# A decode block's tail: w_down with columns as output, the last V piece in two parts, and w_up in one load

## The chip, the cores and the metric

The kernel runs on one core of a Trainium2 chip. The metric is the device time of one execution in microseconds (us), smaller being better. Runs of the kernel before gave 657.47, 657.50 and 658.03 us; the median is 657.5.

## The reference

One token goes through an attention block with a cache of 65,536 positions (32 query heads on 8 key/value heads, 128 per head) and then through a gated layer, both with a residual:

```python
def _A_ref(x, k_cache, v_cache, wq, wo):
    q = (x @ wq).reshape(B, Sq, 32, 128).transpose(0, 2, 1, 3)
    k, v = jnp.repeat(k_cache, 4, axis=1), jnp.repeat(v_cache, 4, axis=1)
    p = _softmax(jnp.einsum("bhqd,bhkd->bhqk", q, k) * 128 ** -0.5)
    o = jnp.einsum("bhqk,bhkd->bhqd", p, v)
    return o.transpose(0, 2, 1, 3).reshape(B, Sq, 4096) @ wo

def _B_ref(x, w_gate, w_up, w_down):            # 512 -> 1792 -> 512
    g, u = x @ w_gate, x @ w_up
    return (_sigmoid(g) * u) @ w_down

h = x + _A_ref(_layernorm(x), k_cache, v_cache, wq, wo)
h2 = h + _B_ref(_layernorm(h), w_gate, w_up, w_down)
```

All inputs and the output of 512 numbers are bf16. The caches are 268 MB of the 282 MB that one execution reads.

## The kernel before

**The stream.** SP issues nearly all loads, in one queue and in a fixed order (L331 to L361): wq, then for each of the eight heads three pieces of K and three of V (12, 8 and 12 chunks of 2048 positions) into a ring of 32 chunks in SBUF, and at the end w_out, the last V pieces, w_gate, w_up and w_down. An issue that has a name in its dependence list waits until the engine that reads the old content of those chunks is done. The last V piece of the last head comes in two loads (`LAST`, L318: chunks 20 to 28 and 28 to 32). Then SP waits for the first six rounds of the last head's PV (L356) and issues w_gate once, w_up twice (three quarters and one quarter, `W_SPLIT`) and w_down three times (`WD_SPLIT`: rounds 0 to 7, 8 to 11, 12 and 13; a round is 128 of the 1792 rows).

**Heads.** DVE transposes K chunks (L511), PE makes scores (L535), DVE takes maxima, ACT the exponentials (L557), DVE transposes these (L567), and PE multiplies them with V in "rounds": one round is two chunks, eight matmuls on four column groups of the array (`pv`, L587). PE's program is a loop written out by hand with registers and branches (`pe_flow`, L669): block `sums` computes the addresses of a round from registers (L582), issues its eight matmuls (section `B`, all through the helper at L430), counts down `m` (L735, L736), and at its end goes on (L738) to `waits` when `k` is not zero. `waits` (L718) sets `m` to the rounds still left, waits for the next V load and goes back to `sums`. A branch that is taken from there for the last piece of V is `fourth` (L727), and for the last head `last_rounds` (L728), which waits for the load of chunks 28 to 32. So the last piece of V of the last head runs four rounds, then `waits`, then two rounds.

**After the heads.** The last head's output is scaled (L600), picked out (L603), regrouped (L616 to L625) and multiplied with the last four rows of w_out, in column form (`project`, L627): the weights are 128x128 slices of w_out with a column stride of four, the moving operand is one column of O, and y comes out as 128 partitions x 4. There follow the residual (L804), the layer norm's sums (L391) and hc, the centred input (L805); its scale, rstd, comes by a short chain on DVE and POOL (L396 to L402). w_gate and w_up are applied in row form on the four column groups (L818): 16 matmuls each, with 448 columns per group. ACT takes tanh of the gate (L825), DVE makes sg2 (L826), the product hh (L828) and its 32x32 transposes hhT (L831), whose columns 32r are the inputs of w_down's round r.

**w_down in row form.** For each of 14 rounds and four column groups, one column of hhT is the weight and 128 columns of w_down move past it (L836); the result is four rows of 128 on partitions 0, 32, 64 and 96. The residual enters the same accumulation by one fp32 matmul (L823) of `gsel`, a selection matrix made at the start (POOL memset L366, DVE reduction L380), with `hz`, a copy of h spread over columns (L807). Two casts on DVE and two on ACT gather the four rows on partition 0 (L840 to L845), and SP stores one row of 512 (L846).

Of the kernel before, what the change touches and what calls it, by code (L numbers as in the profile page):

```python
# [6 lines left out]
bf16 = mybir.dt.bfloat16  # L7
fp32 = mybir.dt.float32
# [5 lines left out]
HKV = 8  # L14
GS = 4
NQ = 32
DH = 128
# [198 lines left out]
def bass_sequential_preLN__gqa_block_cached__glu_gated_glu__decode_kernel(  # L216
# [17 lines left out]
    RW = 4  # L234
    WD_SPLIT = [(0, 8), (8, 12), (12, 14)]
    FG = FF // 4

    with ExitStack() as es:
        def sb(name, shape, dt):
            return es.enter_context(nc.sbuf_tensor(name, shape, dt))  # L240

        gsel = sb("gsel", [128, 128], fp32)
        hz = sb("hz", [128, 128], fp32)
        identf = sb("identf", [128, 128], fp32)
# [27 lines left out]
        qh = sb("qh", [32, 512], bf16)  # L272
        qt = sb("qt", [32, 512], bf16)
        hT = [sb(f"hT{i}", [128, 4], fp32) for i in range(2)]
# [18 lines left out]
        hhT = sb("hhT", [128, FG], bf16)  # L293
        y_sb = sb("y_sb", [1, D], bf16)

# [53 lines left out]
        for i, cols in enumerate(LAST):  # L349
            load("V", h, 2, (), ("vb", "vl")[i], f"V{h}.2{('', 'b')[i]}", cols)  # L350
        for k, w in (("wg", B_w_gate), ("wu", B_w_up)):
# [13 lines left out]
        for nm, t, v in (("onesf", onesf[:, :], 1.0), ("xz0", xz[:, :], 0.0), ("onef", one_f[:, :], 1.0), ("nhalf", nhalf[:, :], -0.5),  # L365
                         ("gs0", gsel[:, :], 0.0), ("zcol", zcol[:, :], 0.0), ("qh0", qh[:, :], 0.0), ("qz0", qz[:, :], 0.0),  # L366
                         ("PTz", PT_sb[:, 4 * 512:PT_ROW], 0.0), ("Wz", ktw[:, W0:KTW_ROW], 0.0)):
            op("pool", lambda e, t=t, v=v: e.memset(t, v), name=nm)
# [101 lines left out]
        op("act", lambda e: e.activation(ps(1, 0, 512, 0, 8), bass.AP(tensor=zcol, offset=0, ap=[[1, 8], [0, 512]]), AF.Copy), ["zcol"], "zq")  # L470
        op("pe", project_q, ["zq", "xz", "wq", "identf", "lsel", "onef", "sel", "gsel", "row", "PTz", "qz0"], "q")
        op("act", lambda e: e.activation(  # L472
# [113 lines left out]

        def pv(h, r, rounds=0):  # L587
            P.part["pe"] = ("B", (h, r, rounds))
            rounds, name = rounds or PARTS[r], f"PV{h}.{r}" + "a" * (rounds == 6)
# [79 lines left out]
        def pe_flow(e, section):  # L669
            later = []  # L670

            def away(op, reg_, value, name, body, back=None):
                getattr(e, op)(reg_, value, on_true=name, on_false=f"{name}_not")
                later.append((name, body, back or f"{name}_not", blocks[-1][0]))
                label(f"{name}_not")

# [41 lines left out]
            def waits():  # L718
                e.reg_alu(m, k, 0, ALU.add)
                e.reg_mov(k, 0)  # L720
                e.br_eq(w, w0, on_true="second", on_false="fourth")
# [5 lines left out]
                e.br_ne(i, i_last, on_true="sums", on_false="last_rounds")  # L727
                label("last_rounds", "fourth")  # L728
                section("VL")

            section("B")
# [5 lines left out]
            label("sums_end")  # L737
            away("br_ne", k, 0, "waits", waits, "sums")  # L738

            away("br_eq", w, w0 - 12, "outs", lambda: section("O"))  # L740
            goto("next", "part")
# [24 lines left out]
        for i in range(HKV + 1):  # L766
            loop, last = 0 < i < HKV, i == HKV
            for r in range(NR):
# [5 lines left out]
                if i and r == 0:  # L774
                    transposed(i - 1)
                    P.part = {"pe": ("V0", i), "dve": ("B0", i) if loop else None}
                    denominators(i - 1)
                    op("pe", lambda e: None, [f"V{i - 1}.0", f"z{i - 1}"])
                    if last:
                        pv(i - 1, r, 6)  # L780
                    P.part["pe"] = ("L" if last else "V2", i)
                    if last:
                        project7()
                        columns()
                    op("pe", lambda e: None, [f"V{i - 1}.1"])
                    pv(i - 1, r, 4 if last else 0)
                if i and r == 3:
                    P.part["pe"] = ("V3", i)
                    op("pe", lambda e: None, [f"V{i - 1}.2"])
                    if last:  # L790
                        P.part["pe"] = ("VL", i)
                        op("pe", lambda e: None, [f"V{i - 1}.2b"])
                    pv(i - 1, r)
                    P.part["pe"] = ("O", i)
                    head_out(i - 1)
                if not last and r == 3:
# [9 lines left out]
                                                   op0=ALU.mult, op1=ALU.add), ["tot.1"], "hc")  # L806
        op("dve", lambda e: e.tensor_tensor(hz[:, :].rearrange("p (j k) -> p j k", k=4),  # L807
                                            bass.AP(tensor=sel_f, offset=0, ap=[[32, 128], [1, 32], [0, 4]]),
                                            bass.AP(tensor=hT[1], offset=0, ap=[[4, 128], [0, 32], [1, 4]]), ALU.mult),
           ["hT.1", "self"], "hz")  # L810
        ln_rstd(1, STB, 0, 4.0)
        wd_v = ring[:, AT["wd"] * CH:AT["wd"] * CH + NF * D].rearrange("p (r n) -> p r n", r=NF)
        for i, (nm, bank) in enumerate((("wg", GB), ("wu", UB))):
            at = W_AT[nm]
            for kt in range(4):
                for c in range(4):
# [11 lines left out]
        op("dve", lambda e: e.tensor_tensor(hh[:, :].rearrange("p (r q) -> p r q", r=NF),  # L828
                                            ps(UB, 0, FG).rearrange("p (q r) -> p r q", r=NF),
                                            sg2[:, :].rearrange("p (q r) -> p r q", r=NF), ALU.mult), ["gu1", "sg2"], "hh")  # L830
        op("dve", lambda e: e.transpose(hhT[:, :], hh[:, :]), ["hh"], "hhT")  # L831
        for i, (r0, r1) in enumerate(WD_SPLIT):
            for r in range(r0, r1):
                for g in range(4):
                    last = r == NF - 1 and g == 3
                    op("pe", lambda e, r=r, g=g: e.matmul(  # L836
                        ps(YB, 0, 128, 32 * g, 32 * g + 1), lhsT=hhT[:, 32 * r:32 * r + 1], rhs=wd_v[:, r, g * 128:(g + 1) * 128],
                        start=False, stop=(r == NF - 1), tile_position=(0, 32 * g), skip_group_check=True),
                       ["hhT", f"wd{i}"] if r == r0 and g == 0 else (), "y" if last else None)
        for g in (0, 2, 1, 3):  # L840
            if g < 2:
                op("dve", lambda e, g=g: e.tensor_copy(y_sb[:, 128 * g:128 * g + 128], ps(YB, 0, 128, 32 * g, 32 * g + 1)), ["y"], f"ysb{g}")
            else:
                op("act", lambda e, g=g: e.activation(y_sb[:, 128 * g:128 * g + 128], ps(YB, 0, 128, 32 * g, 32 * g + 1), AF.Copy),
                   ["y"], f"ysb{g}")  # L845
        dma("sp", lambda e: e.dma_start(out[0], y_sb[:, :]), "out", [f"ysb{g}" for g in range(4)], "out")  # L846
        P.at_end = ("out",)
# [29 lines left out]
```

## Time and profile before

| What | us | Where from |
|---|---|---|
| median of three runs | 657.5 | times |
| the profiled execution | 657.62 | times |
| its span, first to last instruction | 656.2 | page |
| PE busy | 436.0 | page |
| DVE busy | 351.2 | page |
| ACT busy | 42.8 | page |
| last V load of chunks 28 to 32, issue to landing | 38.5 | DMA issues |
| w_up, second part, issue to landing | 34.3 | DMA issues |
| w_down, last part, issue to landing | 37.2 | DMA issues |
| start of the output's DMA issue | 654.99 | timeline |

The profile is of one execution. Times in it count from the first instruction. A row of the timeline gives start, duration, engine, line, operation, output and input, how many instructions it merges, and in brackets how long the engine was idle before it and what ended that. "PEq" is PE's sequencer, which runs branches and register work; "PEld" is the load of weights. A matmul's end is modelled. The granted clock of TensorE changes in steps during the execution; its mean is 0.775 of full speed.

### The profile page before, as it was taken

What the parts mean: (1) busy time and instruction counts of PE and PEld (TensorE: products, weight loads), DVE (VectorE), ACT (ScalarE), POOL (GpSimd) and SP (SyncE); (2) the same over time, 40 slices, a digit from 0 to 9 for tenths busy, and PEclk for the clock granted to TensorE, in tenths of its full rate; (3) what the DMA queues carried; (4) which work ended last, traced back from release to release, by engine and by line L of the source; (5) the groups of instructions that cost most, each with busy time, mean ns of one, the idle gap of its engine ahead of it and who ended that gap; (6) DMA issues with size and microseconds to landing.
All of it is one profiled execution on the core that took longest, in us unless ns stands there. A gap on an engine that the chain in (4) does not pass through costs nothing.

```text
span 656.2 us, 6248 instructions
## 1 busy us (share of the span) xinstructions
PE 436.0 (66%) x2316; PEld 69.4 (11%) x1548; DVE 351.2 (54%) x436; ACT 42.8 (7%) x114; POOL 3.6 (1%) x17
## 2 busy tenths in 40 slices
PE   2698675838658457776676477594667856775855
PEld 1100010001001010010100110010100101001212
DVE  3498836847266645647258380674536572573102
ACT  1100200020000200011000200002000020002001
POOL 1000000000000000000000000000000000000000
PEclk9798688767689587796677676985877967877777
DMA  9999999999999999999999999999999999999998
GB/s 400 431 447 431 425 424 446 437 434 426 441 431 431 431 431 442 437 434 423 423 443 431 431 437 445 437 437 431 415 431 431 431 434 434 457 431 411 439 422 341
DMA packets 8386, 282.33 MB, mean 430 GB/s; under 512 B 961, under 2 KB 962, under 8 KB 1474
## 3 DMA queue, kind: packets, MB, share of 16 engines
q1 hardware_dynamic: 8354, 282.33, 99.6%
q10 hardware_dynamic: 32, 0.00, 0.0%
HBM read 282.33 MB, written 0.00 MB: 430 GB/s over the span
## 4 chain that ended last, share of the span: by engine, by line
DMA 65%; PE 19%; DVE 12%; issue 3%; ACT 1%; SPq 0%; PEldq 0%
DMA ring<-in_A_k_cache_dram 34%; DMA ring<-in_A_v_cache_dram 23%; PE PS L430 18%; DVE ktw L511 11%; DMA ring<-in_B_w_down_dram 6%; DMA ring<-in_A_wq_dram 2%; ACT P_sb L557 1%; DVE PT_sb L567 0%; DVE M_sb L518 0%; SPq L355 0%; PE PS L551 0%; PE PS L544 0%; PEldq L171 0%; SPq L360 0%; PE PS L572 0%
## 5 line engine op out<-in xcount | busy, mean ns | idle before, releaser
L511 DVE STREAM_TRANSPOSE ktw<-ring 128x1024 f32<-128x1024 f32 x256 | 292.4, 1211 | 170.5 <-DMA ring<-in_A_k_cache_dram 170.5
L430 PE MATMUL PS<-ktw 128*128 128x512 bf16 x1024 | 293.2, 438 | 114.8 <-DVE ktw L511 106.7
L430 PE MATMUL PS<-ring,PT_sb 128*32 x1024 | 102.7, 506 | 65.4 <-PEq L171 45.1
L430 PEld LDWEIGHTS PS<-ktw 128*128 x256 | 27.2, 106 | 370.4 <-issue 258.1
L600 ACT ACTIVATE po_sb<-PS,rl 128x512 bf16<-128x512 f32 x8 | 5.5, 687 | 522.2 <-PE PS L430 522.2
L430 PEld LDWEIGHTS PS<-ring,PT_sb 128*32 x1024 | 20.7, 116 | 144.3 <-issue 142.8
L518 DVE TENSOR_REDUCE M_sb<-PS 128x1 f32<-128x512 f32 x32 | 19.9, 684 | 20.0 <-PE PS L430 20.0
L546 DVE TENSOR_REDUCE gmj<-PS 1x4 f32<-1x128 f32 x8 | 2.2, 278 | 40.2 <-PE PS L544 40.2
L557 ACT ACTIVATE P_sb<-PS,negmax 128x512 bf16<-128x512 f32 x32 | 21.5, 685 | 0.3
L567 DVE STREAM_TRANSPOSE PT_sb<-P_sb 128x512 bf16<-128x512 bf16 x32 | 20.2, 688 | 1.7 <-ACT P_sb L557 1.7
L430 PE MATMUL PS<-ring,xz 128*8 x32 | 10.0, 490 | 3.6 <-DMA ring<-in_A_wq_dram 3.6
L616 DVE TENSOR_TENSOR Lw<-O,blk_of 128x896 bf16<-128x896 bf16 (+1 forms) x2 | 1.4, 682 | 19.9 <-ACT O L606 19.9
L544 PE MATMUL PS<-identf,gm 128*1 128x128 f32 x16 | 4.5, 380 | 5.5 <-issue 3.4
L551 PE MATMUL PS<-one_f,gmrep 1*128 1x1 f32 x16 | 4.7, 358 | 5.0 <-DVE gmrep L548 5.0
L574 DVE TENSOR_REDUCE lsum<-PS 128x1 f32<-128x4 f32 x8 | 1.3, 162 | 11.9 <-PE PS L572 11.9
L475 DVE STREAM_TRANSPOSE qt<-qh 32x512 bf16<-32x512 bf16 x1 | 0.7, 699 | 12.7 <-ACT qh L472 12.7
L430 PE MATMUL PS<-ktw,O 128*1 x26 | 7.5, 457 | 0.0
L557 ACT ACTIVATION_READ_ACCUMULATOR P_sb<-PS,negmax 128x1 f32 x32 | 6.5, 203 | 0.0
L603 PE MATMUL PS<-sel_bf,po_sb 128*128 128x4 bf16 x32 | 2.1, 170 | 6.3 <-ACT po_sb L600 6.3
L411 PE MATMUL PS<-xs,xpick 16*128 16x32 bf16 x1 | 0.2, 202 | 7.5 <-DMA xs<-in_A_x_dram 7.5
L572 PE MATMUL PS<-L_sb,lsel 128*128 128x4 f32 x16 | 2.5, 229 | 3.8 <-DVE PT_sb L567 3.8
L661 DVE COPY yr<-PS 1x512 f32<-1x512 f32 x1 | 0.7, 678 | 8.1 <-PE PS L659 8.1
(88 smaller groups left out, 71.6 us busy)
## 6 DMA issues: line engine op xcount, KB each, us to landing
ring<-in_A_k_cache_dram SPq DMA_DIRECT2D x16, 6144.0 KB, 25.4
ring<-in_A_v_cache_dram SPq DMA_DIRECT2D x15, 6144.0 KB, 25.7
ring<-in_A_v_cache_dram SPq DMA_DIRECT2D x9, 4096.0 KB, 30.6
ring<-in_A_k_cache_dram SPq DMA_DIRECT2D x8, 4096.0 KB, 24.7
ring<-in_A_wq_dram SPq DMA_DIRECT2D x1, 4096.0 KB, 12.3
ktw<-in_A_wo_dram SPq DMA_DIRECT2D x1, 3584.0 KB, 14.9
ring<-in_A_v_cache_dram SPq DMA_DIRECT2D x1, 2048.0 KB, 38.5
ring<-in_B_w_gate_dram SPq DMA_DIRECT2D x1, 1792.0 KB, 30.8
```

Of the source, the lines that this page charges most:

```text
L430: return e.add_instruction(mybir.InstMatmult(name=nc.get_next_instruction_name(), engine=mybir.EngineType.PE, ins=[rhs, lhsT], outs=[e.low ...
L511: op("dve", lambda e, d=dst, sr=src: e.transpose(d, sr), deps, f"T{b}.{c}", to="T")
L518: op("dve", lambda e, u=u: e.tensor_reduce(M_sb[:, u % 4:u % 4 + 1], ps(u % NS, 0, 512), AX.X, ALU.max), [f"S{b}.{NC - NR + k}"], f"mx{u}" ...
L544: op("pe", lambda e: e.matmul(ps(MISC, 0, 128, 0, 1), lhsT=gm[:, :], rhs=identf[:, :], start=True, stop=True), [f"gm{h}"], f"gmT{h}", to="Q")
L546: op("dve", lambda e: e.tensor_reduce(gmj[:, :], ps(MISC, 0, 128, 0, 1).rearrange("p (i a c) -> p a i c", a=4, c=NC), AX.XY, ALU.max), [f" ...
L551: op("pe", lambda e: e.matmul(ps(MISC, 128, 129), lhsT=gmrep[0:1, :], rhs=one_f[0:1, 0:1], start=True, stop=True), [f"gmrep{h}"], f"neg{h}")
L557: op("act", lambda e, b=b: e.activation(P_sb[:, (b % 4) * 512:(b % 4 + 1) * 512], ps(b % NS, 0, 512), AF.Exp, bias=negmax[:, k:k + 1], sca ...
L567: op("dve", lambda e, b=b: e.transpose(PT_sb[:, (b % 4) * 512:(b % 4 + 1) * 512], P_sb[:, (b % 4) * 512:(b % 4 + 1) * 512]), [f"E{b}"], f" ...
L572: op("pe", lambda e: e.matmul(ps(MISC, 132, 136), lhsT=lsel[:, :], rhs=L_sb[:, :], start=True, stop=True), [f"PT{NR * h + NR - 1}"], f"l{h ...
L600: op("act", lambda e: e.activation(po_sb[:, :], ps(PO, 0, 512), AF.Copy, scale=rl[:, :]), [f"PV{h}.{NR - 1}", f"rl{h}"], f"po{h}", to="po")
L603: op("pe", lambda e, t=t: e.matmul(ps(OX, 0, 4), lhsT=po_sb[:, t * 128:(t + 1) * 128], rhs=sel_bf[:, 8 * t:8 * t + 8:2], start=(t == 0), s ...
L616: op("dve", lambda e: e.tensor_tensor(Lw[i][:, :].rearrange("p (j c) -> p j c", j=n), bass.AP(tensor=O2, offset=j0, ap=[[NQ, 128], [1, n], ...
```

## The change

- The last V piece is loaded as chunks 20 to 28, 28 and 29, 30 and 31. PE runs four rounds, one round in the loop behind a wait for the second load, and one round, `pv_last`, behind a wait for the third, with addresses that are fixed in the instructions and not taken from registers. After it PE goes straight to the head's output.
- w_up is one load.
- The product hh and its transposes are made in two halves: rounds 0 to 7, and 8 to 13.
- w_down goes in column form, as wo's last rows: 128x128 slices of w_down with a stride of four as weights, one column of hhT as the moving operand, 14 x 4 matmuls into 128 partitions x 4. w_down's loads are rounds 0 to 7, 8 to 10, 11 and 12, 13.
- The residual is added by one DVE operation that also casts; `gsel`, `hz`, their makers, the residual matmul and the four casts go. The output is stored from 128 partitions, four numbers (8 bytes) each.

```diff
-    WD_SPLIT = [(0, 8), (8, 12), (12, 14)]
+    WD_SPLIT = [(0, 8), (8, 11), (11, 13), (13, 14)]
...
-        gsel = sb("gsel", [128, 128], fp32)
-        hz = sb("hz", [128, 128], fp32)
+        qt = sb("qt", [32, 512], bf16)
...
-        y_sb = sb("y_sb", [1, D], bf16)
+        y_sb = sb("y_sb", [128, 4], bf16)
...
-        W_SPLIT = {"wg": [(0, 4)], "wu": [(0, 3), (3, 4)]}
+        W_SPLIT = {"wg": [(0, 4)], "wu": [(0, 4)]}
...
-        LAST = [(20, 28), (28, 32)]
+        LAST = [(20, 28), (28, 30), (30, 32)]
...
-        op("dve", lambda e: e.tensor_reduce(bass.AP(tensor=gsel, offset=0, ap=[[128, 128], [32, 4]]),
-                                            identf[:, :].rearrange("p (s j) -> p s j", s=4), AX.X, ALU.add), ["gs0", "identf"], "gsel")
...
+        def pv_last():
+            for n in (15,):
+                for k in range(2):
+                    for tq in range(4):
+                        lhsT = bass.AP(tensor=PT_sb, offset=(2 * (n % 2) + k) * 512 + 128 * tq + n // 2, ap=[[PT_ROW, 128], [4, 32]])
+                        at = (2 * n + k + first_chunk("V", HKV - 1, 2) - PIECES[2][0]) * CH + 4 * tq * DH
+                        op("pe", lambda e, tq=tq, lhsT=lhsT, at=at: e.matmul(
+                            ps(PO, 0, 512, 32 * tq, 32 * tq + 32), lhsT=lhsT, rhs=ring[:, at:at + 512], start=False, stop=False,
+                            tile_position=(0, 32 * tq), skip_group_check=True),
+                           (), f"PV{HKV - 1}.{NR - 1}" if n == 15 and k and tq == 3 else None)
...
                 label("last_rounds", "fourth")
+                e.br_ne(m, 1, on_true="last_but_one", on_false="last_round")
+                label("last_but_one", "last_rounds")
+                e.reg_mov(m, 1)
+                e.reg_mov(k, 1)
                 section("VL")
+                nc.br("sums", engines=here)
+                label("last_round", "last_rounds")
+                section("VM")
...
-            away("br_ne", k, 0, "waits", waits, "sums")
+            away("br_ne", k, 0, "waits", waits, "outs")
...
-        op("dve", lambda e: e.tensor_tensor(hz[:, :].rearrange("p (j k) -> p j k", k=4),
...
-        op("pe", lambda e: e.matmul(ps(YB, 0, 128), lhsT=gsel[:, :], rhs=hz[:, :], start=True, stop=False, skip_group_check=True), ["hz"])
...
+        HH = ((0, 8), (8, NF))
+        for i, (r0, r1) in enumerate(HH):
+            op("dve", lambda e, r0=r0, r1=r1: e.tensor_tensor(
+                hh[:, 32 * r0:32 * r1].rearrange("p (r q) -> p r q", q=32),
+                ps(UB, 0, FG).rearrange("p (q r) -> p r q", r=NF)[:, r0:r1, :],
+                sg2[:, :].rearrange("p (q r) -> p r q", r=NF)[:, r0:r1, :], ALU.mult), ["gu1", "sg2"], f"hh{i}")
+            op("dve", lambda e, r0=r0, r1=r1: e.transpose(hhT[:, 32 * r0:32 * r1], hh[:, 32 * r0:32 * r1]), [f"hh{i}"], f"hhT{i}")
         for i, (r0, r1) in enumerate(WD_SPLIT):
             for r in range(r0, r1):
-                for g in range(4):
...
+                for nt in range(4):
+                    deps = [f"wd{i}"] if r == r0 and nt == 0 else []
+                    deps += [f"hhT{j}" for j, (h0, _) in enumerate(HH) if r == h0 and nt == 0]
+                    lhsT = bass.AP(tensor=ring, offset=AT["wd"] * CH + r * D + nt, ap=[[RING, 128], [4, 128]])
+                    op("pe", lambda e, r=r, nt=nt, lhsT=lhsT: e.matmul(
+                        ps(YB, nt, nt + 1), lhsT=lhsT, rhs=hhT[:, 32 * r:32 * r + 1], start=(r == 0 and nt == 0),
+                        stop=(r == NF - 1), skip_group_check=True), deps, "y" if r == NF - 1 and nt == 3 else None)
-        for g in (0, 2, 1, 3):
...
-        dma("sp", lambda e: e.dma_start(out[0], y_sb[:, :]), "out", [f"ysb{g}" for g in range(4)], "out")
+        op("dve", lambda e: e.tensor_tensor(y_sb[:, :], ps(YB, 0, 4), hT[1][:, :], ALU.add), ["y"], "ysb")
+        dma("sp", lambda e: e.dma_start(out[0].rearrange("o (p k) -> (o p) k", k=4), y_sb[:, :]), "out", ["ysb"], "out")
```

More of the change, by code (lines that the diff above doesn't have):

```diff
@@ L272, in bass_sequential_preLN__gqa_block_cached__glu_gated_glu__decode_kernel @@
         qh = sb("qh", [32, 512], bf16)
-        qt = sb("qt", [32, 512], bf16)
         hT = [sb(f"hT{i}", [128, 4], fp32) for i in range(2)]
@@ L349, in bass_sequential_preLN__gqa_block_cached__glu_gated_glu__decode_kernel @@
         for i, cols in enumerate(LAST):
-            load("V", h, 2, (), ("vb", "vl")[i], f"V{h}.2{('', 'b')[i]}", cols)
+            load("V", h, 2, (), ("vb", "vl", "vn")[i], f"V{h}.2{('', 'b', 'c')[i]}", cols)
         for k, w in (("wg", B_w_gate), ("wu", B_w_up)):
@@ L365, in bass_sequential_preLN__gqa_block_cached__glu_gated_glu__decode_kernel @@
         for nm, t, v in (("onesf", onesf[:, :], 1.0), ("xz0", xz[:, :], 0.0), ("onef", one_f[:, :], 1.0), ("nhalf", nhalf[:, :], -0.5),
-                         ("gs0", gsel[:, :], 0.0), ("zcol", zcol[:, :], 0.0), ("qh0", qh[:, :], 0.0), ("qz0", qz[:, :], 0.0),
+                         ("zcol", zcol[:, :], 0.0), ("qh0", qh[:, :], 0.0), ("qz0", qz[:, :], 0.0),
                          ("PTz", PT_sb[:, 4 * 512:PT_ROW], 0.0), ("Wz", ktw[:, W0:KTW_ROW], 0.0)):
@@ L470, in bass_sequential_preLN__gqa_block_cached__glu_gated_glu__decode_kernel @@
         op("act", lambda e: e.activation(ps(1, 0, 512, 0, 8), bass.AP(tensor=zcol, offset=0, ap=[[1, 8], [0, 512]]), AF.Copy), ["zcol"], "zq")
-        op("pe", project_q, ["zq", "xz", "wq", "identf", "lsel", "onef", "sel", "gsel", "row", "PTz", "qz0"], "q")
+        op("pe", project_q, ["zq", "xz", "wq", "identf", "lsel", "onef", "sel", "row", "PTz", "qz0"], "q")
         op("act", lambda e: e.activation(
@@ L585, in bass_sequential_preLN__gqa_block_cached__glu_gated_glu__decode_kernel, with pv @@
         PARTS = {0: 10, 3: 6}
-        def pv(h, r, rounds=0):
+        def pv_last():
[8 more added lines that the diff above has]
+                           (), f"PV{HKV - 1}.{NR - 1}" if n == 15 and k and tq == 3 else None)
+        def pv(h, r, rounds=0, part=""):
             P.part["pe"] = ("B", (h, r, rounds))
-            rounds, name = rounds or PARTS[r], f"PV{h}.{r}" + "a" * (rounds == 6)
+            rounds, name = rounds or PARTS[r], f"PV{h}.{r}{part}"
             for k in range(2):
@@ L670, in pe_flow, with away @@
             later = []
-            def away(op, reg_, value, name, body, back=None):
+            def away(op, reg_, value, name, body, back=None, under=None):
                 getattr(e, op)(reg_, value, on_true=name, on_false=f"{name}_not")
-                later.append((name, body, back or f"{name}_not", blocks[-1][0]))
-                label(f"{name}_not")
+                later.append((name, body, back or f"{name}_not", under or blocks[-1][0]))
+                label(f"{name}_not", under)
             i, w, p, v, m, k, s = (R.setdefault(n, e.alloc_register(f"r_{n}")) for n in "iwpvmks")
@@ L737, in pe_flow @@
             label("sums_end")
-            away("br_ne", k, 0, "waits", waits, "sums")
-            away("br_eq", w, w0 - 12, "outs", lambda: section("O"))
+            away("br_ne", k, 0, "waits", waits, "outs")
+            away("br_eq", w, w0 - 12, "outs", lambda: section("O"), under="sums_end")
             goto("next", "part")
@@ L779, in bass_sequential_preLN__gqa_block_cached__glu_gated_glu__decode_kernel @@
                     if last:
-                        pv(i - 1, r, 6)
+                        pv(i - 1, r, 6, "a")
                     P.part["pe"] = ("L" if last else "V2", i)
@@ L790, in bass_sequential_preLN__gqa_block_cached__glu_gated_glu__decode_kernel @@
                     if last:
+                        pv(i - 1, r, 4, "a")
                         P.part["pe"] = ("VL", i)
                         op("pe", lambda e: None, [f"V{i - 1}.2b"])
-                    pv(i - 1, r)
+                        pv(i - 1, r, 1, "b")
+                        P.part["pe"] = ("VM", i)
+                        op("pe", lambda e: None, [f"V{i - 1}.2c"])
+                        pv_last()
+                    else:
+                        pv(i - 1, r)
                     P.part["pe"] = ("O", i)
@@ L832, in bass_sequential_preLN__gqa_block_cached__glu_gated_glu__decode_kernel @@
         for i, (r0, r1) in enumerate(WD_SPLIT):
             for r in range(r0, r1):
-                for g in range(4):
[L835 to L839, printed above, removed]
```

13 lines of the change are left out of this document (removed).

## The prediction

> **What bounds the kernel now.** I read the page's chain of work first, then the chain in order of time near the end, then the timeline of the last 20 us, then rows of single source lines. The page:
>
> ```profile
> span 656.2 us, 6248 instructions
> PE 436.0 (66%) x2316; PEld 69.4 (11%) x1548; DVE 351.2 (54%) x436; ACT 42.8 (7%) x114; POOL 3.6 (1%) x17
> DMA  9999999999999999999999999999999999999998
> q1 hardware_dynamic: 8354, 282.33, 99.6%
> ```
>
> No engine is near full, but the DMA queue is busy for 99.6% of the span. The kernel is a 282 MB stream with work hidden under it, and only what follows the stream's last byte, or what makes the stream stop, can move the time. The end of the chain (start us, us, what):
>
> ```profile
> 616.72 37.16 DMA ring<-in_B_w_down_dram
> 653.88 0.04 issue
> 653.92 0.41 PE PS L836 x7
> 654.33 0.02 issue
> 654.35 0.09 DVE y_sb L842
> 654.44 0.22 issue
> 654.66 0.28 DVE y_sb L842
> ```
>
> The last piece of w_down lands at 653.88. Eight matmuls, two casts in a row and the output's DMA follow: 2.35 us to the end of the span. The compute that runs up to that point, by the timeline (start, us, engine, line, what, count, idle before and its releaser):
>
> ```profile
> 598.57 0.63 PE L430 MATMUL PS<-ring,PT_sb 128*32 x8 [1.24 <-issue]
> ...
> 636.76 3.82 PE L430 MATMUL PS<-ring,PT_sb 128*32 x32 [6.04 <-PEq L171]
> 641.68 0.63 PE L430 MATMUL PS<-ring,PT_sb 128*32 x8 [1.10 <-DMA ring<-in_A_v_cache_dram]
> 642.65 0.63 PE L430 MATMUL PS<-ring,PT_sb 128*32 x8 [0.34 <-issue]
> ...
> 645.41 0.69 PE L632 MATMUL PS<-O,ktw 128*128 128x1 bf16 x16 [0.26 <-DVE O L625]
> ...
> 647.59 3.09 PE L818 MATMUL PS<-ring,hc 128*1 128x448 bf16 x32 [0.25 <-DVE hc L805]
> ...
> 650.74 0.92 DVE L828 TENSOR_TENSOR hh<-PS,sg 128x448 bf16<-128x448 f32 x1 [0.31 <-PE PS L818]
> 651.69 0.65 DVE L831 STREAM_TRANSPOSE hhT<-hh 128x448 bf16<-128x448 bf16 x1
> 652.39 0.62 PE L836 MATMUL PS<-ring,hhT 128*1 128x128 bf16 x32 [1.29 <-DVE hhT L831]
> ```
>
> Two things are to be seen. The compute is only 0.2 us ahead of the stream: the 32 matmuls that start at 652.39 are done at 653.01, and the next w_down piece lands at 653.25 (issued at 616.24, 37.0 us). And the 1.10 us before round 5 of the last V piece, though put down to a DMA, is no larger than the 1.24 us that the same place takes at 598.57, where the whole piece had long landed: it is the sequencer's. The piece that round 5 waits for (issued at 602.42, 38.5 us to landing) was there at 640.9, while the sequencer was still in its branches:
>
> ```profile
> L721 PEldq COMPARE_BRANCH  x1: 207/207/207, 640.7 to 640.7; - x1
> L727 PEldq COMPARE_BRANCH  x1: 72/72/72, 640.9 to 640.9; - x1
> L753 PEldq COMPARE_BRANCH  x1: 177/177/177, 641.1 to 641.1; - x1
> ```
>
> **The change, part by part.** Sums are made against the profiled execution: 657.62 us, of which 656.2 are the span and 1.4 lie outside it; the median of the runs shown is 657.5.
>
> *Start.* POOL loses the memset of gsel (0.31 us at 1.38), DVE its reduction (0.28 us at 3.90). Both stand ahead of PE's first matmul, which starts at 7.53 and waited 7.5 us for x. Cost 0; without x's wait it would be a gain of 0.3 at most. q starts when wq lands at 13.0, so the stream is not touched.
>
> *SP's queue.* V's last piece becomes two issues (+1, 0.43 us, at 602.9); behind it SP waits 11.6 us for PE at 614.45, which hides it. Behind that wait there are six issues as before (w_gate, w_up once instead of twice, w_down four instead of three). Bytes and their order stay, so landings stay: V's parts at 636.15 (issued at 601.95, 34.2 us), about 638.6 (half of the 4.8 us between the two old landings) and 640.9; w_up whole at 649.59 (its second part was issued at 615.29 and took 34.3 us); w_down's end at 653.88.
>
> *Last V piece.* Four rounds from 636.76 as before, then the branches up to L727. New after L727 and ahead of round 5: a comparison that falls through (0.13 us, as L727 at 640.94 to L753 at 641.07) and two register moves (0.24 us: L719 at 640.44 to L721 at 640.68): round 5 starts at 641.68 + 0.37 = 642.05. Its landing, 638.6, is no longer in play, and was not before. Round 6 was a turn of the loop, 0.97 us after round 5. Now round 5 leaves the loop and goes through the same branches: from round 4's first matmul (639.71) to the start after L727 (641.07) is 1.36 us, plus a comparison that jumps (L721's 207 ns, 0.27 us to the next instruction), and then matmuls with no register work: 1.63 us. Round 6 starts at 643.68 instead of 642.65: **+1.03 us**, and queued behind it are po (L600), wo's last rows, the layer norm and the gate and up products. Bounds: +1.24 (the 598.57 gap, taken whole for the second exit in place of 0.34, and the 0.37) and, if the landing were what round 5 waits for, -0.3.
>
> *w_up whole.* Up's first weights went at 648.67, on a part that landed at 648.5; now they need 649.59. With the 1.0 us from above they go at 649.70, so this wait is covered; if the V edit cost nothing, this one would hold up by 0.95 us. So up's end at 650.68 becomes 651.6 to 651.7 either way, and the two prices are paid once: **+1.0 us at hh**.
>
> *Halves.* 915 ns and 645 ns for 448 columns are 2.04 and 1.44 ns each: 0.52 + 0.37 us for the first 256, 0.39 + 0.28 for the other 192. From 651.74: the first transposed half is there at 652.66, the second at 653.39 (0.03 us between, as at 651.69).
>
> *w_down as columns.* 56 matmuls with 128x128 weights and one moving column. The nearest row is L632, the same form and stride, at clock 0.50: 16 in 0.69 us, so (0.69 - 0.17) / 15 = 35 ns each, against 4 at a time in the old form (32 in 0.62 us). From 652.71, 32 take 1.12 us; by 653.83 the second half is there; the remaining 24 take 0.84 and the last ends 0.14 later: 654.81, and the stream's end at 653.88 is no longer what they wait for. The old end was 654.30. Bounds: 14 ns each, the old row's, gives 654.2, where the last landing decides (653.92, four matmuls); 58 ns each, from L622 (7 in 0.54 us, another stride), gives 656.1.
>
> *Output.* The residual matmul (0.49 us at 650.61, in PE's idle time) and hz go. Two casts in a row (654.35 to 654.94) become one add of 128x4; L804, the same add, took 0.16 us. 654.81 + 0.05 + 0.16 + 0.05 = 655.07 for the issue against 654.99: **+0.1 us**, with bounds -0.5 and (58 ns) +1.3. Then the DMA: one packet of 1024 B, issued at 654.99, moved at 655.74, and SP was released at 656.21. Now it is 128 rows of 8 B. No such DMA is in the trace. Nearest rows: the wq load, also 128 rows on an idle queue, whose first packets start 1.03 us and whose last engine starts 1.75 us after its issue at 0.00, against 0.75 for the output's one packet; and x's 16 packets of 64 B, 0.011 us each. From below: +0.3 (first packets 0.28 later, 8 packets of 0.011 per engine). From above: +1.0 for the last engine, and 8 packets at the 0.047 us that the 1024 B packet took: +1.4. I take **+0.7**, between them, since the wq row is the program's first DMA and may be late for that.
>
> The Trainium skill, "DMA: Bandwidth & Descriptors", section Specifications, speaks against this edit: a transfer below 512 B is done as a read-modify-write. No run here shows a small write to HBM; by this rule the price would lie toward the upper bound, 1.4. The same page, section "Anatomy of one DMA — SWDGE (gpsimd) path", says that many descriptors can be emitted before their cost shows; by that it would be near nothing, and the 1.03 to 1.75 us of wq do not agree with it.
>
> Sum: 657.62 + 0.1 + 0.7 = 658.4, and 658.3 from the median of 657.5.
>
> **Rivals.**
> 1. *The output's rows are free.* For it: descriptors are made while the engine idles, and eight packets of 0.011 us are 0.09 us. Against it: wq's late engines. 657.5 + 0.1 + 0.1 = 657.7.
> 2. *The end becomes the stream's.* If columns go at 14 to 20 ns (the clock was granted 1.00 from 650.70 to 653.90, 0.50 at L632), PE waits for the last landing: issue at 654.46, -0.5; with the output at +0.3, 657.3. Against it: L632's 35 ns are from weight loads of this shape, and the only faster rows load one column.
> 3. *Slower: the 8-byte writes.* Place: between the issue and SP's release, where nothing hides it. It decides from 1.2 us above the old 1.22, with the +0.1. At its upper bound: 657.5 + 0.1 + 1.4 = 659.0. For it: last engine at 1.75, and all 16 write into the same 1 KB. Against it: the wq row's spread may be a cold start.
> 4. *The split does what its words say* and PV ends earlier. Against it: the landing came before the branch. It would change little: up then waits for w_up at 649.59, and the issue comes at 655.0. 658.2 with the forecast's output.
>
> **How the numbers follow.** A measurement of this kernel tells about 0.2%, 1.3 us, from no change. Forecast (with rival 4, which shares its output price) 0.45, rival 1 0.17, rival 2 0.12, rival 3 0.26. Faster by over 1.3 us would need more than half of the 2.35 us after the last landing, of which 1.22 are the output's DMA: 0.06, out of rival 2. Slower takes rival 3, whose upper bound is just over the limit, and a slow column form: 0.27. The rest, 0.67, is within. The range reaches from rival 2 without an output price (657.0) to rival 3 with 0.3 us of slower columns (659.3).
>
> **What would show it.** In the new profile: round 5 at about 642.05 and round 6 near 643.7, po 1.0 us later; up's weights at about 649.7 with no long wait for w_up; two transposes of 0.37 and 0.28; 56 column matmuls at 35 ns ending near 654.8 with no wait for w_down after the first; one add of 0.16; issue near 655.1, and 1.9 us from there to the end of the span instead of 1.22. It is wrong if round 6 starts before 643, if the matmuls wait for the last piece, or if the output takes under 1.4 or over 2.5 us.

## The result, and the profile after

The changed kernel took **660.19 us** (median of 7 runs, 659.74 to 660.50) against 657.56 us for the kernel before (7 runs, 657.45 to 658.53). The ratio is 1.0037, with a 95% interval of 1.0026 to 1.0048: slower by 2.6 us, above the predicted 658.3 and above the range's end at 659.3. The profiled execution took 660.08 us, 658.7 of them the span; before it was 657.62 and 656.2. So 2.5 us were lost inside the span, and the 1.4 us outside it stayed.

The page after. Below "DMA" come the queues: packets, MB, share of the 16 engines' span.

```profile
span 658.7 us, 6241 instructions
DMA  9999999999999999999999999999999999999996
q1 hardware_dynamic: 8640, 282.33, 99.3%
q14 instruction: 2, 0.01, 0.0%
q8 instruction: 1, 0.02, 0.0%
```

The stream moves the same 282.33 MB; the last slice is emptier (6 instead of 8), so the time went behind the stream's end. Two lines are new. One is a packet of 16 KB on a queue for instructions, q8. The other is q14, whose 8 KB packet comes at the end of the kernel before too, but behind its span (656.91). The end of the chain, in order of time (start us, us, what):

```profile
648.85 3.19 PE PS L833 x32
652.04 0.02 issue
652.06 0.59 DVE hh L844
652.66 0.02 issue
652.68 0.46 DVE hhT L848
653.14 0.14 issue
653.27 2.01 PE PS L855 x56
655.29 0.03 issue
655.31 0.16 DVE y_sb L858
```

Before, this chain began with w_down's DMA, landed at 653.88. Now no DMA is in it: w_down's last part lands at 653.81 in the landings' record, and PE works on until 655.27. What set the chain's times stands in the timeline of after (start, us, engine, line, what, count, idle before it and its end):

```profile
636.55 3.85 PE L426 MATMUL PS<-ring,PT_sb 128*32 x32 [5.50 <-PEq L171]
...
641.84 0.63 PE L426 MATMUL PS<-ring,PT_sb 128*32 x8 [1.43 <-issue]
...
643.47 1.05 PE L589 MATMUL PS<-ring,PT_sb 128*32 128x512 bf16 x8 [1.00 <-issue]
644.58 0.69 ACT L607 ACTIVATE po_sb<-PS,rl 128x512 bf16<-128x512 f32 x1 [38.41 <-PE PS L589]
...
655.50 0.35 SPq L859 DMA_DIRECT2D out_dram<-y_sb  x1
```

Rounds 5 and 6 are eight matmuls each. Round 6 starts 6.92 us after round 1; before it was 5.89 (642.65 - 636.76). The difference is 1.03 us, and no wait for a load stands ahead of either round. The output's issue is at 655.50, only 0.51 us later than before. The other 2 us are behind it, by the view of the output's tensor:

```profile
L859 SPq DMA_DIRECT2D out_dram<-y_sb x1: 348/348/348, 655.5 to 655.5; - x1
...
DMA to landing us min/median/max: 3.2/3.2/3.2
```

From issue to landing 3.2 us pass, where 1.12 passed before (1.22 to SP's release). The packet records of this execution show two things in that time. The 8-byte packets of 15 DMA engines had moved by 656.54, but their landings are spread over 656.75 to 658.69. The last eight moved only from 657.59, right behind the 16 KB packet of q8 (656.53, 1.07 us), so I take them for the sixteenth engine's. So there were two suspects: the small writes (W below), and the instruction fetch (F below), which could come from PE's longer program. The built PE program has 494 words (instructions and labels) after and 476 before.

### The profile page after: what moved, and what is told of

It is laid out like the page before. It is cut to its first block, busy times and chain, and to the rows that moved or that the text cites. A ratio compares the mean times of both kernels' runs of the same rounds, so it can differ in the third digit from the quotient of the medians.

```text
span 658.7 us, 6241 instructions
## 1 busy us (share of the span) xinstructions
PE 436.3 (66%) x2314; PEld 70.2 (11%) x1546; DVE 350.6 (53%) x435; ACT 42.3 (6%) x112; POOL 3.4 (1%) x16
## 3 DMA queue, kind: packets, MB, share of 16 engines
q1 hardware_dynamic: 8640, 282.33, 99.3%
HBM read 282.33 MB, written 0.00 MB: 429 GB/s over the span
```

## The experiments

The kernel before took 657.66 (18 runs), 657.62 (30) and 657.60 us (29) beside them. The first column of times is the median.

| Run | PE's words | output stored as | us | ratio to before, 95% | issue at |
|---|---|---|---|---|---|
| e1 changed kernel | 494 | 1 row | 660.35 | 1.0022 to 1.0049 | 655.55 |
| e2 changed kernel | 494 | 16 x 64 B | 660.11 | 1.0022 to 1.0049 | 655.54 |
| e3 before | 476 | 128 x 8 B | 659.46 | 1.0017 to 1.0037 | 655.10 |
| e4 changed, V not split | 473 | 128 x 8 B | 659.71 | 1.0020 to 1.0039 | 654.61 |
| e5 before, 18 PE instructions more | 494 | 1 row | 659.19 | 1.0012 to 1.0030 | 655.39 |
| e6 before, V split | 497 | 1 row | 659.57 | 1.0020 to 1.0041 | 656.06 |
| e7 changed, V not split | 473 | 1 row | 657.36 | 0.9987 to 1.0005 | 654.53 |
| e8 before, one cast | 476 | 4 x 256 B | 657.75 | 0.9991 to 1.0009 | 654.42 |
| e9 e7, 18 PE instructions more | 491 | 1 row | 660.97 | 1.0027 to 1.0055 | 654.67 |
| e10 e1, last round in the loop | 480 | 1 row | 658.91 | 1.0011 to 1.0028 | 656.25 |
| e11 changed, V not split | 473 | 64 x 16 B | 658.04 | 0.9998 to 1.0015 | 654.58 |
| e12 changed, V not split | 473 | 16 x 8 B | 658.26 | 1.0001 to 1.0019 | 654.71 |

**e1, e2, e3: the output's form alone.** e1 and e2 store other rows of the right size from the changed kernel, e3 stores 128 small rows from the kernel before:

```diff
 e1
-        dma("sp", lambda e: e.dma_start(out[0].rearrange("o (p k) -> (o p) k", k=4), y_sb[:, :]), "out", ["ysb"], "out")
+        dma("sp", lambda e: e.dma_start(out[0], qz[0:1, 0:512]), "out", ["ysb"], "out")
 e2
+        dma("sp", lambda e: e.dma_start(out[0].rearrange("o (p k) -> (o p) k", k=32), qz[0:16, 0:32]), "out", ["ysb"], "out")
 e3
-        dma("sp", lambda e: e.dma_start(out[0], y_sb[:, :]), "out", [f"ysb{g}" for g in range(4)], "out")
+        dma("sp", lambda e: e.dma_start(out[0].rearrange("o (p k) -> (o p) k", k=4), qz[:, 0:4]), "out", [f"ysb{g}" for g in range(4)], "out")
```

> The changed kernel, but the output's store takes one row of 512 numbers from partition 0 of another tile, still behind the add; the stored numbers are not the result. Theory W (the 128 rows of 8 bytes are slow to be written): issue to the end of the span falls from 3.2 us to about 1.2 as in the kernel before, so 660.2 - 2.0 = 658.2 us. Rival F (the store is held by an instruction fetch of 16 KB that runs on one of the DMA engines from 656.53 to 657.60 in the changed profile): issue to end stays at about 3 us or falls to no less than 2.2, and the time stays above 659.2. Rival C (the store's form costs little, the compute ahead of it is what is late in the unprofiled runs): 660 us.

> The changed kernel, but the store takes 16 rows of 64 bytes from another tile, still behind the add; the stored numbers are not the result. Theory W in its form 'a price for each row written': an eighth of the rows, so (3.2 - 1.2) / 8 = 0.25 us above the one row's 1.2, about 658.5 us. Theory W in its form 'a price for any row below 512 bytes, paid once': about 2 us more than one row, 660 us. Rival F: issue to end near 3 us whatever the rows.

> The kernel before, with one thing changed: the store takes 128 rows of 8 bytes from another tile, behind the same four casts; the stored numbers are not the result. Theory W: issue to end 3.2 us in place of 1.2, 657.6 + 2.0 = 659.6 us. Rival F (the fetch belongs to the changed program's longer code): 657.6 to 658.0 us.

e3 is slower than before by 1.8 us with nothing but the small rows. Its output, by the view of its tensor:

```profile
DMA to landing us min/median/max: 3.0/3.0/3.0
```

Here there is no packet on q8, and the span is 658.1: W alone costs 1.8 us, inside the span (two of the nine runs have 2.0 and 2.5 us outside it, the others 1.3 to 1.4). But e1, where W is undone, did not come back: 660.35. The page's first line of e1, and below it the queues at its end (the view of the DMA from 640 us on):

```profile
span 656.8 us, 6241 instructions
```

```profile
q8 instruction: 1, 0.02, 0.3%
q14 instruction: 1, 0.01, 0.1%
issues: line engine op xcount, KB each, median us to landing
out_dram<-qz SPq DMA_DIRECT2D x1, 1.0 KB
```

The span ends 1.9 us earlier than in the changed kernel, yet the execution took 660.37: 3.6 us lie outside the span instead of 1.4. The row had landed at 656.67, 1.12 us after its issue. Of the five signals at the barrier behind the span four came at 656.97 to 657.09 and the fifth at 659.33, after a 16 KB fetch that ran from 656.65 to 657.94. All five runs of e1 have 2.5 to 3.9 us outside the span. e2 has the same fetch (656.60 to 658.00): 15 of 16 landings of its 64 B rows came by 656.87, and the last, whose packet moved only at 657.98, at 659.08. So rows of 64 B do not pay W, and there is a second price, F, which the changed kernel pays in the same microseconds.

**e4, e7: without the V split.** e4 is the changed kernel with the last V piece as before; e7 stores one row besides.

```diff
-        LAST = [(20, 28), (28, 30), (30, 32)]
+        LAST = [(20, 28), (28, 32)]
...
-                        pv(i - 1, r, 1, "b")
-                        P.part["pe"] = ("VM", i)
-                        op("pe", lambda e: None, [f"V{i - 1}.2c"])
-                        pv_last()
+                    pv(i - 1, r)
```

> The changed kernel with the last V piece as before: two loads, four rounds and two rounds in the loop. Theory P (the exit from the loop after round 5 costs 1.0 us on the path to the end, and the wait for the whole w_up takes its place when it is gone): round 6 back to 5.9 us after round 1 from 6.9, up's weights wait for w_up until about 649.6, and the output's issue comes 0.2 to 0.6 us earlier than at 655.50; 659.7 us. Rival: w_up is not waited for and the whole 1.0 us comes back, 659.2 us. Rival: the PV rounds were hidden and nothing comes back, 660.2 us.

> The changed kernel without the V split and with the output as one row of 512 numbers from another tile (the stored numbers are not the result). PE's program is 3 instructions shorter than before's. Theory W with F2: issue at about 654.6, end of span 655.8, and the time 657.2 us, or up to 658.2 if the late fetch that the run without the split showed (time minus span 2.3 us) is there without the slow writes. Rival (the column form itself is what costs): 659 us or more.

The timeline of e4:

```profile
641.58 0.63 PE L426 MATMUL PS<-ring,PT_sb 128*32 x8 [1.13 <-DMA ring<-in_A_v_cache_dram]
642.55 0.63 PE L426 MATMUL PS<-ring,PT_sb 128*32 x8 [0.34 <-issue]
...
649.46 1.66 PE L809 MATMUL PS<-ring,hc 128*1 128x448 bf16 x16 [0.30 <-DMA ring<-in_B_w_up_dram]
652.39 2.00 PE L831 MATMUL PS<-hhT,ring 128*128 128x1 bf16 x56 [1.26 <-DVE hhT L824]
```

Round 6 is back in its old place, and now up waits for w_up, as the prediction said of this case. The issue is 0.9 us earlier than in the changed kernel. Of the 0.9 us, 0.42 are round 6 itself, which took 0.63 us here and 1.05 in the changed kernel. The time is hardly earlier: 659.71. W is still paid (2.8 us from issue to landing), and that is not all: the profiled run has 2.4 us outside its span, and a 16 KB packet of q8 from 658.72 to 659.99, though PE's program is shorter than before's. Six of the ten runs have 2.1 us or more outside the span; the other four, with 1.3 to 1.4, took 658.75 to 659.14. So e4 is not free of F. The queues at its end:

```profile
q14 instruction: 1, 0.01, 0.6%
q8 instruction: 1, 0.02, 0.3%
```

With both undone, e7 takes 657.36, and a difference from before can't be told (two of its eleven runs have 2.1 and 2.4 us outside the span). Undoing W alone gains nothing (e1), undoing the V split alone 0.5 us (e4), both 2.8 us (e7). The two prices are not simply added: they lie side by side at the end.

**e5, e6, e9, e10: is F the V split's branches, or the length of PE's program?** e5 and e9 add nine matmuls (18 PE instructions) whose result nothing reads, to the kernel before and to e7. e6 is the V split alone on the kernel before. e10 is e1 with its last round as a turn of the loop, so that the split stays but PE's program is short.

```diff
 e5, e9
+        for i in range(9):
+            op("pe", lambda e: e.matmul(ps(OX, 8, 12), lhsT=ident[:, :], rhs=sel_bf[:, 0:4], start=True, stop=True))
 e10
+                e.reg_mov(m, 1)
...
-            away("br_ne", k, 0, "waits", waits, "outs")
+            away("br_ne", k, 0, "waits", waits, "sums")
...
-                        pv_last()
+                        pv(i - 1, r, 1)
```

> The kernel before plus nine small matmuls whose result nobody reads, placed where PE waits for hhT: 18 instructions more in PE's program, as the changed kernel has 16 more. Theory F2 (PE's longer program makes the end of the execution wait for a 16 KB instruction fetch, as in the run with one output row, where the span was 656.8 us and the time 660.4): the span stays within 0.3 us of 656.2, and the time rises to 659.3 to 660.2, so time minus span goes from 1.4 to over 3 us. Rival (the length of the program is free): 657.5 to 657.9 us.

> The kernel before with the split of the last V piece alone. Theory P with F2: round 6 is 6.9 us after round 1 in place of 5.9, the span rises by 0.2 to 0.6 us, and the time by about 2.3 us more than a normal end gives: 659.5 to 660.3 us. Rival P alone (no price beyond the branches): 657.8 to 658.2 us.

> The changed kernel without the V split, its output stored as one row taken from x's tile (so the output is not y), which took 657.36 us, plus nine unread matmuls (18 PE instructions) in PE's wait for the gate product; nothing waits for them. Theory F (a PE program that is some 16 instructions longer makes an engine fetch 16 KB more of it, which ends 1 to 2 us after the last store): 658.8 to 660, with the SP issue where it was (654.5) and the fifth barrier signal or the span's end late. Rival (the length is innocent; what cost e1 its 2.6 us are the V split's branches and its third landing): 657.2 to 657.6.

> The changed kernel with its V split in three landings, but the last round through the loop's registers like the others (no round at fixed addresses: PE's program is 14 instructions shorter than the changed kernel's and 4 longer than before), and the output stored as one row taken from x's tile (not y). Round 6 should start about 1 us after its place before, as in the changed kernel. Theory F: the SP issue at 655.3 to 655.8, no late barrier, 658.0 to 658.5. Rival (the split's branches or its landing make the end late, whatever the length): 659.8 to 660.4, as e1.

The length alone costs 1.6 us in e5 and 3.6 us in e9, more than expected there; neither has a V split, nor small rows. The page's first line of e9, and the queues at its end:

```profile
span 656.0 us, 6258 instructions
```

```profile
q8 instruction: 1, 0.02, 0.2%
q14 instruction: 1, 0.01, 0.1%
```

This execution took 661.22 us: 5.2 us outside a span of 656.0. Five of six runs of e9 took 660.9 to 661.2, one 658.1, so the price isn't paid in full every time. Its first five barrier signals are on time; the sixth, 0.8 us behind the fifth in the kernel before, comes 4.7 us behind it, at 660.97, and the 16 KB packet ran from 657.91 to 658.84.

In e5 the 16 KB packet came at 655.28, and all eleven runs have 2.5 to 3.5 us outside the span. The trace points to the engine that was late there: in each of the other 13 profiled kernels the first of the signals at the end comes 0.17 to 0.19 us behind PE's last matmul, in e5 3.1 us behind it (657.79 against 654.71).

e10 is the counter-test. The queues at its end, and its timeline:

```profile
q1 hardware_dynamic: 891, 5.58, 55.4%
q14 instruction: 1, 0.01, 0.1%
```

```profile
636.68 4.01 PE L426 MATMUL PS<-ring,PT_sb 128*32 x32 [5.54 <-PEq L171]
...
641.91 1.05 PE L426 MATMUL PS<-ring,PT_sb 128*32 x8 [1.22 <-issue]
...
644.24 1.05 PE L426 MATMUL PS<-ring,PT_sb 128*32 x8 [1.28 <-issue]
```

No q8, span 657.5, time 658.88: 1.4 us outside, as before. The split and its branches are there, so they alone don't cause F. The median of 658.91 is above the 658.0 to 658.5 expected, and the timeline says why: a round behind the loop's exit and its register work starts 2.33 us after the one before it, where the fixed addresses took 1.63. I had left these 0.7 us out. Against e1 it is still 1.4 us faster, though it issues 0.7 us later.

e6 is less clear: 659.57, but in two groups (658.6 to 659.3 and 659.9 to 660.3). In its profiled run (658.61) the 16 KB packet came in mid-stream, at 620.98. After it the loads landed over 1.7 to 1.8 us instead of the 0.5 ahead of it, because one DMA engine stayed about 1.1 us behind the others, and the stream ended at 655.04. Round 1 started at 637.90, 1.1 us later than before, so the issue at 656.06 holds that delay as well as the split's 1.03 us (round 6 at 644.82, 6.92 us after round 1), and e6 doesn't tell the one from the other. It suggests that the fetch can cost about a microsecond without standing at the end.

**e8, e11, e12: what makes a small write dear?** e8 gathers the row form's four rows by one cast and stores 4 x 256 B. e11 and e12 are e7 with 64 rows of 16 B and 16 rows of 8 B.

```diff
 e8
+        y_sb = sb("y_sb", [128, 128], bf16)
...
+        op("dve", lambda e: e.tensor_copy(y_sb[:, :], ps(YB, 0, 128)), ["y"], "ysb")
+        dma("sp", lambda e: e.dma_start(out[0].rearrange("o (g n) -> (o g) n", n=128), bass.AP(tensor=y_sb, offset=0, ap=[[32 * 128, 4], [1, 128]])),
+            "out", ["ysb"], "out")
 e11
+        dma("sp", lambda e: e.dma_start(out[0].rearrange("o (p k) -> (o p) k", k=8), qz[0:64, 0:8]), "out", ["ysb"], "out")
 e12
+        dma("sp", lambda e: e.dma_start(out[0].rearrange("o (p k) -> (o p) k", k=4)[0:16], qz[0:16, 0:4]), "out", ["ysb"], "out")
```

> The kernel before with the four casts replaced by one DVE cast of 128x128 (the rows between are not stored) and the store from partitions 0, 32, 64 and 96 in four rows of 256 bytes. If four short rows cost as little as one and the cast takes 0.28 us, the issue comes 0.3 us earlier: 657.3 us. If each short row is slow, as theory W in its form 'any row below 512 bytes' has it: 658 us or more.

> The changed kernel without the V split, its output stored as 64 rows of 16 B from x's tile (so the output is not y). One row took 1.12 us from issue to landing, 128 rows of 8 B 2.8 us. If each small write beyond what the 16 DMA engines take at once costs its turn (count): 1.7 to 2.2 us and a time of 657.9 to 658.6. If the price is that of 8-byte rows alone (size): 1.1 to 1.3 us and 657.2 to 657.6.

> The changed kernel without the V split, storing only 16 rows of 8 B from x's tile (128 B; the rest of the output is not written). Count: 1.1 to 1.3 us from issue to landing, 657.2 to 657.6. Size (an 8-byte write is slow by itself): above 2 us and 658.3 or more.

e8 issues 0.57 us earlier than before: 0.32 because one cast stands where two followed each other, and 0.25 because PE itself was done earlier in this execution (654.05 against 654.30). But its issue takes SP 0.66 us instead of 0.33, and its landing comes 1.66 us after the issue's start instead of 1.12. The time is that of before. From issue to landing, by the views of the output's tensor, e11 and then e12:

```profile
DMA to landing us min/median/max: 1.7/1.7/1.7
```

```profile
DMA to landing us min/median/max: 1.3/1.3/1.3
```

The expectations' two forms of W, a price by the count of rows and one by their size, are told apart by splitting this time at the first packet, by the packets' and the landings' records (us; the first two columns count from the start of the issue):

| Output | issue takes | first packet at | from there to the last landing |
|---|---|---|---|
| 1 x 1024 B (before) | 0.33 | 0.75 | 0.37 |
| 4 x 256 B (e8) | 0.66 | 1.25 | 0.41 |
| 16 x 8 B (e12) | 0.36 | 0.86 | 0.48 |
| 64 x 16 B (e11) | 0.56 | 1.20 | 0.52 |
| 128 x 8 B (e3) | 0.35 | 0.84 | 2.13 |

e11 took the 1.7 us that the count foretold, but not for that reason: it is 0.4 us longer than e12 mainly because its first packet came 0.34 us later, behind a longer issue, and its 16 landings stand within 0.16 us, like e12's. Only 128 rows of 8 B have landings far apart (1.72 us from the first to the last in e3, 1.52 in e4). So neither the size alone (e12) nor a count of 64 (e11) makes W; between e11 and e3 both the size and the count change, and in e3, e11 and e12 every row also comes from a partition of its own, so what makes the last step isn't shown. e12's time, 658.26, is 0.9 us above e7's. It lies above the 657.2 to 657.6 of the count and, by 0.04, under the 658.3 of the size, and most of the 0.9 is outside the span: ten of its eleven runs have 1.9 to 2.9 us there, e7 1.4. In every record an 8 KB packet on q14 comes at the end. It took 1.84 us in e12, 1.27 in e11, 2.40 in e3 and e4, 1.99 in the changed kernel, but 0.32 before and 0.42 to 0.53 behind one row, 4 x 256 B or 16 x 64 B. So behind rows of 8 and 16 B the instruction fetch that follows is slower. That is read from one record each; why, isn't shown.

## Why the prediction was wrong

The predicted sum ended at 658.4 for an execution like the profiled one, which took 660.08. Its 0.1 us up to the issue measured 0.51, and its 0.7 from the issue to the span's end 2.0 (3.22 against 1.24). By its own terms:

- **The V split's branches: right.** +1.03 us was predicted for round 6 against round 1, and 1.03 was measured; rounds 5 and 6 were put at 642.05 and 643.68 and started at 641.84 and 643.47 (rounds 1 to 4 ran 0.2 us earlier in this execution). The landings are not what either waits for.
- **w_up whole: the wait right, its size too large.** No wait for w_up after; in e4, without the split, there is one, of 0.30 us. The prediction put up's end at 651.6 to 651.7 with the split or without it, so that the split had no price of its own. With it the end was 652.0, without it 651.12 (649.46 + 1.66). 0.42 us of that difference are round 6's duration; the other 0.5 the split did cost.
- **Halves: too small by 0.3 us.** 0.52, 0.37, 0.39 and 0.28 us were scaled from 448 columns in proportion; 0.58, 0.45, 0.45 and 0.38 were measured. An operation has a fixed part (0.07 us for the product, 0.17 for the transpose, by the straight line through 256 and 192 columns), which proportion leaves out. Only the first half's 0.14 us reaches the issue: the 56 matmuls do not wait for the second half.
- **Round 6's duration: not in the sum.** It took 1.05 us instead of 0.63, since its clock was low there. The windows of before and after (us, PE busy, PEld, DVE, ACT, POOL, granted clock, DMA share, GB/s):

```profile
642.60:643.30 0.70, 0.63 (x8) 0.16 (x8) 0.00 (x0) 0.00 (x0) 0.00 (x0) 1.00 1.05 451
```

```profile
643.40:644.60 1.20, 1.05 (x8) 0.15 (x8) 0.00 (x0) 0.02 (x1) 0.00 (x0) 0.53 1.01 430
```

  The granted clock was 1.00 before and 0.53 after. It isn't the split's doing: in e9, without a split, the same two rounds had 0.50, and in e6, with it, they took 0.63 each. In the changed kernel round 5 had 1.00 and took 0.63.
- **Columns at 35 ns: right**, 56 in 2.00 us against 1.96 + 0.14, with no wait for w_down after the first. Its issue was put at 655.07 and came at 655.50: the halves and the clock, less the 0.2.
- **The output's DMA: the step that failed.** "I take +0.7, between them", with an upper bound of +1.4, in place of the 1.22 us from issue to release: 1.9 us predicted, 3.2 measured, above the 2.5 that was named as the sign of a wrong prediction. e3 measured the edit by itself at +1.8. The bound took the spread of wq's engines and the packets' own time (8 of 0.047 us per engine). But in e3, without a fetch, all packets had moved 1.04 us after the issue, and what took the time came behind them: landings that are spread over 1.72 us, for which the prediction had no term. Rival 3 had the right place and the right sign, and was given 0.26; its price was too low by the same bound. The Trainium skill, "DMA: Bandwidth & Descriptors", section Specifications, spoke against the edit, rightly; but by its limit of 512 B the rows of 64 B and of 256 B should have paid too, and from the first packet on they landed nearly as fast as one row (0.47 us in e2, but for the row behind the fetch, and 0.41 in e8, against 0.37). The other section of the Trainium skill that the prediction cites there is on the gpsimd path, and this store was issued by SP.
- **What the prediction hadn't seen: F.** It took the 1.4 us that "lie outside" the span as a constant and gave PE's 16 more instructions no price but their branches. Undoing the output alone (e1) left the time at 660.35 with 3.6 us outside the span. Had W cost 0.7, the time would still have been near 660, by e1. The Trainium skill, "Runtime: NRT & Kernel Launch", section Instruction fetch mechanics, says that programs are fetched in blocks of 16 KiB, 256 instructions each, that this is mostly hidden, and that a taken branch to a block that is not loaded makes the engine wait. The blocks agree with q8's packet of 16 KB, and hidden it was not here; whether a branch was the reason, no run here shows.

What is shown: that 18 unread PE instructions cost 1.6 to 3.6 us (e5, e9), that the split costs them only with its fixed round (e1 against e10), and that 128 rows of 8 B alone cost 1.8 us (e3). A late end is not new with the longer program: 12 of the 77 runs of the kernel before and two of e7's eleven (476 and 473 words) have 1.9 to 2.6 us outside the span instead of 1.3 to 1.7. With 491 and 494 words every run of e1, e5 and e9 is late, by 2.3 to 5.4 us outside the span; the changed kernel and e2 pay in the same microseconds as the output. No run of e8 and e10 (476 and 480 words) is late.

What is argued: that the packet on q8 is PE's program and is the reason. The times fit, and e5's late signal points to PE, but the record doesn't say whose packet it is, and e4 and e7, with 473 words, have one too (e7's from 655.44 to 656.87, with the barrier on time). A longer program also moves the places of its branches' targets, and no run here changes the one without the other. So the added instructions turn a price that some runs paid before into one that all pay; by which step stays open, as does why e9 pays twice what e5 does.

Nothing that ran beats the kernel before. Of what the change was made of, the column form, the halves, the whole w_up and the single add are worth 0.46 us at the issue (654.53 in e7 against 654.99), and the store from 128 partitions costs four times that. A version that first gathers the columns into a few rows was not tried.

## What to carry to other kernels

Cost an output by the form in which it is stored, not by its bytes: a column form that saves half a microsecond of compute is lost if it ends in 128 rows of 8 B. After adding instructions to a long engine program, look outside the span as well as in it, over several runs. Where undoing one suspect changes nothing, undo two at once, since prices that lie side by side hide each other.

## What the runs showed of the hardware

- 18 instructions that nothing waits for made a 657.4 us kernel take 661.0 in five of six runs; a 16 KB instruction packet took 0.92 to 1.42 us, and in the changed kernel and in e2 the last of the output's packets moved only behind it (657.59 and 657.98).
- Behind a fetch in mid-stream (e6, 620.98) one engine's share of every later load landed about 1.1 us late, to the stream's end.
- From issue to landing a 1 KB row took 1.12 us and 128 rows of 8 B 2.8 to 3.0, with landings spread over 1.5 to 1.7 us; 64 rows of 16 B and 16 of 8 B landed within 0.16 us. Behind rows of 8 and 16 B the 8 KB fetch took 1.3 to 2.4 us instead of 0.3 to 0.5.
- A cast of four partitions' rows stored as 4 x 256 B took SP 0.66 us to issue, twice what one row (0.33) or 128 rows (0.35) took.
